# Adaptive layer norm, S4D convolution and a token mixer on one core: where the input's row groups are loaded, when their statistics are taken, and how many products of ones TensorE makes in the first cycle

## The chip, the core and the metric

The kernel runs on one core of one Trainium2 chip. The core has TensorE (PE, the matrix engine), VectorE (DVE), ScalarE (ACT), GpSimd (POOL) and SyncE (SP). SP only issues DMA transfers here, and GpSimd issues some beside its arithmetic. Each engine works through its own list of instructions in order and waits on semaphores for what others make. PE has a second lane in the profile, PEld, for weight loads. The metric is device time in microseconds (us). The kernel before took 697.01 us, the median of three runs (696.69 to 698.48).

## The reference, cut to what matters

```python
x = A_u                                                   # 2048 x 448, fp32
mod = (silu(c) @ w_mod).reshape(1, 6, 1, 448)
sa, ca, ga, sb, cb, gb = six rows of mod
h = layernorm(x) * (1 + ca) + sa
x = x + ga * S4D(h)            # long convolution with a kernel K, by FFT
h = layernorm(x) * (1 + cb) + sb
x = x + gb * mixer(h)          # (W2 gelu(W1 layernorm(h)^T))^T, over the token axis

# S4D: dt = exp(log_dt);  A = -exp(log_A_real) + i A_imag;  C = (C_real + i C_imag) dt
# K[d, l] = 2 Re sum over n of C[d, n] exp(A[d, n] dt[d] l)       d < 448, n < 256, l < 2048
# y = irfft(rfft(h) rfft(K))[:2048] + h D_skip
# mixer: 2048 -> 1792 -> 2048, weights w1 and w2
```

All the change touches is in the first tenth of the run: the first layer norm's statistics of x, and the making of K beside it.

## The kernel before

**Making K.** K is made in 56 steps `s` (28 groups of 16 channels, two halves of the 256 states). A step needs exponents and phases as products of small tables on PE, exponentials and sines of them on ACT, the factors `E` and `G` as elementwise products on DVE and GpSimd, and 64 small products `kg<-E,G` on PE that add them up over the states. Eight steps make a cycle (`BATCH`). A cycle begins with `window(s)`: PE makes the exponents of all eight steps (`xe`, `xg <- tab,lex`, L627) and ACT takes their exponentials (`mag`, L650), one table of functions for all of them. Then each step of the cycle runs `st_step`: ACT takes two absolute values and four sines (L683 to L688), DVE makes `E` in four instructions (L692, L693, L695, L696) and GpSimd makes `G` in two (L690, L691). PE makes the phases of the next step (`st_phase`, L627 with `lph`), and the 64 products of the step before the last (`st_kgen`, L717). The phases stand in two pairs of PSUM banks that DVE reads when it makes `E`, so the phases of step s + 1 wait until `E` of step s - 1 is done. `st_mag2` (GpSimd, L666 and L671) makes a product of magnitudes that `E` reads.

**Before the first cycle** a chain of small instructions on DVE, ACT and GpSimd (`first_chain`) turns the parameters of the first 128 channels into pairs of high and low parts. SP moves them straight into the small tables `lex` and `lph` (`direct`, L885), and also stores them to DRAM (`pars`, L889), from where later groups are loaded (L613, L617). A second chain for the next channels (`chain(1)`) is dealt out in single instructions on DVE (`more`).

**The input.** `x_load(r0, n, eng)` (L306) loads row groups r0 to r0 + n - 1 of x into `xt`, in four transfers of 32 partitions, by the engine given, SP if none is. There are 16 row groups, and each is 224 KB over its four transfers. Row groups 0 to 3 are issued by GpSimd inside `first_chain`, 4 to 7 by SP ahead of the first cycle in two calls of two groups, and 8 to 15 by GpSimd behind steps 1 and 2. `u_stats(r)` (L519, L520) takes mean and variance of row group r on DVE. Groups 0 to 3 are taken inside `window(0)`, the others between the second and third `E` instruction of steps 2 to 7, two in each (`between`). All 16 must be there when `window(8)` computes the scale of the layer norm (`logs(True)`, `u_scale`), from which GpSimd makes `wur` (L535) and PE the first stage of the transform of x (`pu`, L548).

**Other names.** `wm_load(k, tile)` (L331) loads 784 KB of w_mod, and `late[s]` holds loads that SP issues ahead of step s. `modulation` (L504, L508) are PE products on them. `warm(n)` (L639) makes n products of ones on PE into a part of the bank `kg` that nobody reads.

**What sets the order.** PE, ACT, DVE and GpSimd run in the order in which the code is written. So does SP up to step 8. Up to eight of SP's transfers are under way at once, since each waits for the one eight places ahead of it.

Of the kernel before, what the change touches and what calls it, by code (L numbers as in the profile page):

```python
# [30 lines left out]
BATCH = 8  # L31
# [195 lines left out]
def tile_adaln_s4d_mixer(ctx, tc, i, out):  # L227
# [20 lines left out]
    with ExitStack() as es:  # L248
        V, S, G, T = nc.vector, nc.scalar, nc.gpsimd, nc.tensor
# [93 lines left out]
        def wm_slot(k):  # L343
# [3 lines left out]


        late = {
            4: lambda: wm_load(2, wm_slot(2)),  # L350
            7: lambda: wm_load(0, wm_slot(0)),
            6: lambda: [
                nc.sync.dma_start(wu, i["WU"]),
# [309 lines left out]
        def st_mag2(s):  # L663
            me = v32(mags[s][:, 0])
            w = wp.tile([P, GD], F32, tag="w", name="w")
            G.tensor_tensor(w[:, :, None], me[:, :, 31:32], me[:, :, 1:2], ALU.mult)  # L666
            if s in (3, 4, 5):
                m2 = v32(wm0.rearrange("p k d -> p (k d)")[:, -512 * (s - 2) :][:, 0:512])
            else:
                m2 = m2p[s >= 32 and s % BATCH > 2].tile([P, GD, 32], F32, tag="m2", name="m2")  # L670
            G.tensor_tensor(m2, me, w[:, :, None].to_broadcast([P, GD, 32]), ALU.mult)  # L671
            m2s[s] = m2
# [190 lines left out]
        def first_chain():  # L863
            cr, ci, a, aim = (raws[0][nm] for nm in ("A_C_real", "A_C_imag", "A_log_A_real", "A_A_imag"))
            xa, ya, s, t, u, ph, p64 = (
                qp.tile([P, N], F32, tag=nm, name=nm) for nm in ("xa", "ya", "s", "t", "u", "ph", "p64")
            )

            w = xp.tile([P, 2, D], F32, tag="yt", name="first", bufs=3)[:, 0, 0:N]

            def split(eng, src):

                hl = room.pop()
                eng.tensor_copy(hl[:, 0].bitcast(F32R), src)
                eng.tensor_tensor(hl[:, 1].bitcast(F32R), src, hl[:, 0], ALU.subtract)
                return hl

            room = wm0.rearrange("p k d -> p (k d)")[:, -12 * N :].rearrange("p (h j n) -> p h j n", h=6, j=2)
            room = [room[:, h] for h in range(6)]
            signs = room.pop()  # L880
            sr, si_ = signs[:, 0], signs[:, 1]

            def direct(hl, tile, r, g):

                nc.sync.dma_start(tile[g][r : r + 32].bitcast(F32), hl[16 * g : 16 * g + 16])  # L885

            def store(hl, *places):
                for k, v in places:
                    nc.sync.dma_start(pars[0][v, k], hl)  # L889

            S.activation(xa, cr, AF.Abs, scale=0.5)
            S.activation(ya, ci, AF.Abs, scale=0.5)
            S.activation(a, a, AF.Exp, bias=ldt0)
            S.activation(dt[:, 0:1], ldt0, AF.Exp)

            S.activation(one, one, AF.Ln)

            ts(sr, cr, 0.0, 0.5, ALU.is_ge, ALU.subtract)
            ts(si_, ci, 0.0, 0.5, ALU.is_ge, ALU.subtract)
            tt(s, xa, ya, ALU.add)  # L900
            tt(ya, ya, xa, ALU.subtract)
            ts(s, s, 2.0**-120, None, ALU.max)
            V.reciprocal(xa, s)
            ha = split(G, a)
            tt(ya, ya, xa, ALU.mult)
            ts(t, s, 2.0**-40, 2.0**80, ALU.is_lt, ALU.mult)
            stt(p64, t, 1.0, s, ALU.max, ALU.mult)
            for g in range(4):
                direct(ha, lex, 0, g)
                if g < 3:  # L910
                    direct(ha, lex, 64, g)
            par_load(1, par_names[0:2])
            x_load(0, 4, G)
            S.activation(u, ya, AF.Square)
            S.activation(u, u, AF.Ln, bias=1.0)
            S.activation(p64, p64, AF.Ln)
            S.activation(xa, ya, AF.Arctan)
            S.activation(xa, xa, AF.Copy, scale=4 * i2p, bias=-0.5)
            S.activation(dt[:, 1:4], ldt[:, 1:4], AF.Exp)
            S.activation(sc, cvec, AF.Exp, scale=-1.0)  # L920

            ts(dt4[:, 0:1], dt[:, 0:1], 1.0 / (4 * math.pi), None, ALU.mult)
            ts(ldt2[:, 0:1], ldt0, 1.5 * math.log(2.0), None, ALU.add)
            ts(ph, aim, dt4[:, 0:1], None, ALU.mult)
            ts(w, ph, MAGIC, MAGIC, ALU.add, ALU.subtract)
            stt(s, t, -80 * math.log(2.0) / 2.0**80, p64, ALU.mult, ALU.add)
            stt(s, u, 0.5, s, ALU.mult, ALU.add)
            ts(s, s, ldt2[:, 0:1], None, ALU.add)
            hs = split(V, s)
            for g in range(4):  # L930
                direct(hs, lex, 96, g)
                if g == 0:
                    direct(ha, lex, 64, 3)
            tt(ph, ph, w, ALU.subtract)
            hp = split(G, ph)
            direct(hp, lph, 0, 0)

            ts(w, ph, MAGIC7, MAGIC7, ALU.add, ALU.subtract)
            tt(p64, ph, w, ALU.subtract)

            tt(xa, xa, sr, ALU.mult)
            stt(xa, xa, 0.5, si_, ALU.add, ALU.mult)
            stt(xa, ph, 63.0, xa, ALU.mult, ALU.add)
            ts(u, xa, MAGIC, MAGIC, ALU.add, ALU.subtract)
            tt(xa, xa, u, ALU.subtract)
            store(ha, (0, 1), (1, 1))
            hl = split(G, p64)
            direct(hl, lph, 64, 0)
            hc = split(V, xa)
            direct(hc, lph, 96, 0)  # L950
            store(hs, (2, 1))
            store(hp, (0, 0))
            store(hl, (1, 0))
            store(hc, (2, 0))
# [2 lines left out]
        par_load(1, par_names[2:4])  # L957
        for g in (1, 2):
            load(g, False)
        x_load(4, 2)  # L960
        x_load(6, 2)
        wm_load(1, wm_slot(1))
        remainder()

# [44 lines left out]
        def window(s):  # L1009
# [11 lines left out]
            for e in range(BATCH):  # L1021
                st_exp(s + e)

                if e + 1 < BATCH:
                    st_exponents(s + e + 1)
                else:
                    st_phase(s)
                mellow()
                flush(dve)
                flush(act)  # L1030
                if s == 8 and e == 0:
                    tt(mod[1], mod[1], mod[2], ALU.mult)
                if s < 32:
                    more(WPACE[s // 8][e])
                if s == 0 and e >= 4:
                    u_stats(e - 4)
                if s == 8 and e in (3, 4):
                    modulation(0, e - 3)
                if s == 8 and e == 5:

                    G.tensor_tensor(mod[0], mod[0], mod[2], ALU.mult)
                if s and e < (2 if s <= 32 else 1):
                    st_kgen(s - (2 if s <= 32 else 1) + e)
                elif e == 5:
                    if s == 8:
                        yks[0] = y0.tile([P, 32, DC], F32, tag="yk", name="yk0")
                    st_s1(s > 16)

                for k, e0 in ((4, 1), (5, 3), (3, 6)) if s == 16 else ():
                    if e in (e0, e0 + 1):  # L1050
                        modulation(k, e - e0)

                if s == 8:
                    warm(7)
                if s in (8, 16):
                    some(u_rows, rows, (2, 2, 2, 2, 2, 0, 1, 1)[e])
                elif s == 24 and e != 5:
                    some(u_cols, cols, 1)

                if s >= 40 and e == 2:  # L1060
                    piece(False, True)
                if s >= 40 and e == 4:
                    piece(pieces[0] < NP, True)
                if s == 0 and e > 1:
                    st_mag2(e - 2)
                elif s and (e < 2 or s >= 32):
                    st_mag2(s + e)
                if s == 0 and e == 3:
                    for r in range(4):
                        dsk_copy(r)  # L1070
# [10 lines left out]
        for s in range(tail):  # L1081
# [21 lines left out]
            def between():  # L1103
                flush(dve)
                if 2 <= s < BATCH:
                    for r in range(2 * s, 2 * s + 2):
                        u_stats(r)
                if s < len(pace):
                    more(pace[s])
# [5 lines left out]
            else:  # L1115
                if s < 32 and s % BATCH > 1:
                    st_kgen(s - 2)
                if s % BATCH < 2:
                    warm(10)
                if (s + 1) % BATCH:  # L1120
                    st_phase(s + 1)
                elif s + 1 < NHALF:
                    st_exponents(s + 1)
# [8 lines left out]
                st_kgen(s - 1)  # L1132


            if s in (1, 2):
                x_load(4 + 4 * s, 4, G)
            free = s > 7 and not st_s1(s % BATCH == BATCH - 1)
            if s + 2 < 32 and (s + 2) % BATCH > 1 and s + 2 > 5:
                st_mag2(s + 2)
# [325 lines left out]
```

## Time and profile before

| | |
|---|---|
| median of three runs | 697.01 us |
| the profiled execution's own time | 694.39 us |
| its span, first to last instruction | 692.6 us |
| PE busy | 643.8 us (93%) |
| DVE, ACT, POOL busy | 428.5, 451.4, 279.0 us |
| mean granted TensorE clock | 0.989 |

A row of the timeline has a start and a duration in us, the engine, the line of the kernel, the operation, what it writes and reads, how many instructions are merged into the row (x), and in brackets how long the engine had been idle before it and what ended that. "issue" is time in which the profile shows nothing that the engine waited for. A row of waits has a total, how often, and the longest. In a table of stretches stand the busy time of each engine in a stretch, the granted clock, the busy share of the 16 DMA engines and what they moved in GB/s.

### The profile page before, as it was taken

What the parts mean: (1) busy time and instruction counts of PE and PEld (TensorE: products, weight loads), DVE (VectorE), ACT (ScalarE), POOL (GpSimd) and SP (SyncE); (2) the same over time, 40 slices, a digit from 0 to 9 for tenths busy, and PEclk for the clock granted to TensorE, in tenths of its full rate; (3) what the DMA queues carried; (4) which work ended last, traced back from release to release, by engine and by line L of the source; (5) the groups of instructions that cost most, each with busy time, mean ns of one, the idle gap of its engine ahead of it and who ended that gap; (6) DMA issues with size and microseconds to landing.
All of it is one profiled execution on the core that took longest, in us unless ns stands there. A gap on an engine that the chain in (4) does not pass through costs nothing.

```text
span 692.6 us, 18551 instructions
## 1 busy us (share of the span) xinstructions
PE 643.8 (93%) x7332; PEld 487.5 (70%) x7332; DVE 428.5 (62%) x818; ACT 451.4 (65%) x848; POOL 279.0 (40%) x367
## 2 busy tenths in 40 slices
PE   0868999999988899999999999999999999999997
PEld 0444454455445676676789767778899999999996
DVE  7877889787575684857745477776732364444431
ACT  5887698899879899999767578787322352222220
POOL 6694669588488777777568000000000000000000
PEclk9998999999999999999999999999999999999999
DMA  7695647588785585554589699966574445555540
GB/s 181 180 208 134 213 168 239 219 229 272 218 266 166 146 165 162 152 151 120 163 271 358 188 262 251 246 153 162 168 229 112 142 133 160 160 169 166 168 123 27
DMA packets 99496, 128.14 MB, mean 185 GB/s; under 512 B 13518, under 2 KB 79986, under 8 KB 99410
## 3 DMA queue, kind: packets, MB, share of 16 engines
q1 hardware_dynamic: 98210, 123.42, 62.8%
q0 software_dynamic: 1200, 3.54, 2.3%
q8 instruction: 58, 0.95, 0.6%
q14 instruction: 28, 0.23, 0.1%
HBM read 91.57 MB, written 34.87 MB: 183 GB/s over the span
## 4 chain that ended last, share of the span: by engine, by line
PE 72%; ACT 9%; DVE 5%; DMA 4%; issue 4%; POOL 2%; SPq 2%; DVEq 0%; ACTq 0%; POOLq 0%
PE xe L627 8%; PE o L1432 7%; PE o L1431 6%; PE o L1433 6%; PE acc L1270 6%; PE acc L1271 6%; PE acc L1272 6%; PE kg L717 6%; PE xg L627 3%; PE vv L836 3%; PE kx L820 3%; PE vv L837 3%; PE pu L548 3%; PE pu L580 2%; PE kg L639 2%
## 5 line engine op out<-in xcount | busy, mean ns | idle before, releaser
L212 ACT CAST whi<-w 128x896 fp32r<-128x896 f32 x64 | 59.6, 938 | 131.2 <-PE o L1432 82.7
L221 DVE TENSOR_TENSOR wlo<-w,whi 128x896 fp32r<-128x896 f32 x64 | 68.1, 1086 | 40.2 <-ACT whi L212 37.0
L690 POOL TENSOR_TENSOR G<-mag,gs 128x512 f32<-128x512 f32 x56 | 71.9, 1284 | 49.7 <-ACT gs L686 49.7
L1270 PE MATMUL acc<-h3h,whi 128*128 128x448 f32 x224 | 83.0, 371 | 0.7 <-ACT u L1398 0.7
L1271 PE MATMUL acc<-h3l,whi 128*128 128x448 f32 x224 | 81.3, 363 | 0.0
L1432 PE MATMUL o<-ul,whi 128*128 128x448 f32 x224 | 81.3, 363 | 0.0
L1431 PE MATMUL o<-uh,whi 128*128 128x448 f32 x224 | 81.2, 362 | 0.0
L1272 PE MATMUL acc<-h3h,wlo 128*128 128x448 f32 x224 | 80.6, 360 | 0.0
L1433 PE MATMUL o<-uh,wlo 128*128 128x448 f32 x224 | 80.6, 360 | 0.0
L717 PEld LDWEIGHTS kg<-E,G 128*32 128x32 f32 x3584 | 55.4, 113 | 30.4 <-issue 20.0
L691 POOL TENSOR_TENSOR G<-mag,gs 128x512 f32<-128x512 f32 x56 | 71.9, 1283 | 0.0
L717 PE MATMUL kg<-E,G 128*32 128x64 f32 x3584 | 64.8, 225 | 4.8 <-issue 4.0
L627 PE MATMUL xg<-tab,lph 64*128 64x512 f32 x112 | 62.9, 561 | 5.5 <-ACT gs L687 2.9
L627 PE MATMUL xe<-tab,lph 64*128 64x512 f32 x112 | 62.3, 556 | 1.1 <-ACT gs L687 0.9
L692 DVE TENSOR_TENSOR E<-m,xe 128x512 f32<-128x512 f32 x53 | 36.3, 685 | 40.4 <-ACT xe L685 20.4
L1436 DVE TENSOR_TENSOR y<-o,x 128x448 f32<-128x448 f32 x16 | 10.0, 627 | 78.8 <-PE o L1433 78.8
L671 POOL TENSOR_TENSOR m<-mag,w 128x512 f32<-128x512 f32 x53 | 55.8, 1053 | 4.2
L1270 PEld LDWEIGHTS acc<-h3h,whi 128*128 128x128 f32 x224 | 42.0, 188 | 14.2 <-ACT h L1335 4.2
L627 PE MATMUL xe<-tab,lex 64*128 64x512 f32 x56 | 28.7, 527 | 17.5 <-DMA lex<-wm 16.4
L828 DVE TENSOR_TENSOR z<-kx,u 128x448 f32<-128x448 f32 x48 | 28.4, 619 | 26.7 <-PE kx L820 26.7
L1431 PEld LDWEIGHTS o<-uh,whi 128*128 128x128 f32 x224 | 42.1, 188 | 3.1
L1272 PEld LDWEIGHTS acc<-h3h,wlo 128*128 128x128 f32 x224 | 41.9, 187 | 3.1
(242 smaller groups left out, 1531.1 us busy)
## 6 DMA issues: line engine op xcount, KB each, us to landing
w<-in_B_w_dram SPq DMA_DIRECT2D x64, 224.0 KB
w<-in_B_w_dram SPq DMA_DIRECT2D x32, 448.0 KB
yu_d<-yt SPq DMA_DIRECT2D x16, 448.0 KB
yi<-yu_d SPq DMA_DIRECT2D x32, 224.0 KB
us_d<-uo SPq DMA_DIRECT2D x16, 448.0 KB
u<-us_d SPq DMA_DIRECT2D x32, 224.0 KB
v_d<-vt SPq DMA_DIRECT2D x32, 224.0 KB
vt<-v_d SPq DMA_DIRECT2D x14, 448.0 KB
```

Of the source, the lines that this page charges most:

```text
L212: self.nc.scalar.copy(hi, w)
L221: eng.tensor_tensor(lo, w, hi.bitcast(F32), ALU.subtract)
L627: T.matmul(out[k], lhs[r], rhs[r], start=start, stop=stop)
L690: G.tensor_tensor(Gt[:, 1], mg_, v32(sg), ALU.mult)
L691: G.tensor_tensor(Gt[:, 0], mg_, v32(cg_), ALU.mult)
L717: T.matmul(kg[32 * q : 32 * q + 32, m], Gt[:, c, d], E[:, c, d], start=h == 0 and c == 0 and m == 0, stop=h == 1 and c == 1, skip_group_ch ...
L1270: nc.tensor.matmul(acc[f], hi[:, fs], h3h[:, r], start=r == 0, stop=False)
L1271: nc.tensor.matmul(acc[f], hi[:, fs], h3l[:, r], start=False, stop=False)
L1272: nc.tensor.matmul(acc[f], lo[:, fs], h3h[:, r], start=False, stop=r == 15)
L1431: nc.tensor.matmul(o, hi[:, ks], uh[kh][:, k], start=kh == 0 and k == 0, stop=False)
L1432: nc.tensor.matmul(o, hi[:, ks], ul[kh][:, k], start=False, stop=False)
L1433: nc.tensor.matmul(o, lo[:, ks], uh[kh][:, k], start=False, stop=kh == 1 and k == 6)
```

## The change

Row groups 0 to 3 are still loaded by GpSimd, but from inside `window(0)`: the four transfers are issued between the two instructions of `st_mag2(0)`. SP issues groups 4 to 7 and 8 to 11 where it issued 4 to 7, in two calls of four groups, and groups 12 to 15 ahead of step 3, behind a w_mod load that moves there from step 4. GpSimd issues nothing behind steps 1 and 2 any more. The statistics of groups 4 to 15 are taken in other steps: 2, 3, 2, 2, 2 and 1 of them in steps 2 to 7. In steps 2 to 7 PE makes four products of ones between `st_kgen` and `st_phase`, and in the first part of `window(8)` 16 in place of 7.

```diff
--- before.py
+++ after.py
@@ -347,7 +347,7 @@
 
 
         late = {
-            4: lambda: wm_load(2, wm_slot(2)),
+            3: lambda: [wm_load(2, wm_slot(2)), x_load(12, 4)],
             7: lambda: wm_load(0, wm_slot(0)),
             6: lambda: [
                 nc.sync.dma_start(wu, i["WU"]),
@@ -664,6 +664,8 @@
             me = v32(mags[s][:, 0])
             w = wp.tile([P, GD], F32, tag="w", name="w")
             G.tensor_tensor(w[:, :, None], me[:, :, 31:32], me[:, :, 1:2], ALU.mult)
+            if s == 0:
+                x_load(0, 4, G)
             if s in (3, 4, 5):
                 m2 = v32(wm0.rearrange("p k d -> p (k d)")[:, -512 * (s - 2) :][:, 0:512])
             else:
@@ -910,7 +912,6 @@
                 if g < 3:
                     direct(ha, lex, 64, g)
             par_load(1, par_names[0:2])
-            x_load(0, 4, G)
             S.activation(u, ya, AF.Square)
             S.activation(u, u, AF.Ln, bias=1.0)
             S.activation(p64, p64, AF.Ln)
@@ -957,8 +958,8 @@
         par_load(1, par_names[2:4])
         for g in (1, 2):
             load(g, False)
-        x_load(4, 2)
-        x_load(6, 2)
+        x_load(4, 4)
+        x_load(8, 4)
         wm_load(1, wm_slot(1))
         remainder()
 
@@ -1051,7 +1052,7 @@
                         modulation(k, e - e0)
 
                 if s == 8:
-                    warm(7)
+                    warm(7 if e else 16)
                 if s in (8, 16):
                     some(u_rows, rows, (2, 2, 2, 2, 2, 0, 1, 1)[e])
                 elif s == 24 and e != 5:
@@ -1103,7 +1104,7 @@
             def between():
                 flush(dve)
                 if 2 <= s < BATCH:
-                    for r in range(2 * s, 2 * s + 2):
+                    for r in ((4, 5), (6, 7, 8), (9, 10), (11, 12), (13, 14), (15,))[s - 2]:
                         u_stats(r)
                 if s < len(pace):
                     more(pace[s])
@@ -1117,6 +1118,8 @@
                     st_kgen(s - 2)
                 if s % BATCH < 2:
                     warm(10)
+                elif s < BATCH:
+                    warm(4)
                 if (s + 1) % BATCH:
                     st_phase(s + 1)
                 elif s + 1 < NHALF:
@@ -1132,8 +1135,6 @@
                 st_kgen(s - 1)
 
 
-            if s in (1, 2):
-                x_load(4 + 4 * s, 4, G)
             free = s > 7 and not st_s1(s % BATCH == BATCH - 1)
             if s + 2 < 32 and (s + 2) % BATCH > 1 and s + 2 > 5:
                 st_mag2(s + 2)
```

On GpSimd, the end of `first_chain` and the start of `window(0)`. `wm_79` is the room for high and low parts, `ph`, `p_192` and `A_log_A_real` are parameters of the first chain, `mag` holds the exponentials and `m_330` the product that step 0 reads. Before:

```order
L875 TENSOR_TENSOR wm_79<-A_log_A_real,wm_79 128x256
L306 DMA xt<-in_A_u_dram 32x4x448 x4
L874 CAST wm_79<-ph 128x256
L875 TENSOR_TENSOR wm_79<-ph,wm_79 128x256
L874 CAST wm_79<-p_192 128x256
L875 TENSOR_TENSOR wm_79<-p_192,wm_79 128x256
L666 TENSOR_TENSOR w<-mag 128x16
L671 TENSOR_TENSOR m_330<-mag,w 128x512
```

The same place with the change:

```order
L877 TENSOR_TENSOR wm_79<-A_log_A_real,wm_79 128x256
L876 CAST wm_79<-ph 128x256
L877 TENSOR_TENSOR wm_79<-ph,wm_79 128x256
L876 CAST wm_79<-p_192 128x256
L877 TENSOR_TENSOR wm_79<-p_192,wm_79 128x256
L666 TENSOR_TENSOR w<-mag 128x16
L306 DMA xt<-in_A_u_dram 32x4x448 x4
L673 TENSOR_TENSOR m_330<-mag,w 128x512
```

The four loads moved behind two more splits and behind `w` of step 0, which waits for the first exponential of ACT.

On SP, from the loads of x ahead of the first cycle to the loads for the second. `lph` and `lex` are tables of phases and exponents, `pars_57` the parameters stored in DRAM, `wm_79` here the room of w_mod:

```order
-L306 DMA xt<-in_A_u_dram 32x2x448 x8
+L306 DMA xt<-in_A_u_dram 32x4x448 x8
 L331 DMA wm_79<-in_w_mod_dram 112x4x448
 L613 DMA lph_142<-pars_57 32x256
 L617 DMA lph_142<-pars_57 64x1x256
+L331 DMA wm_79<-in_w_mod_dram 112x4x448
+L306 DMA xt<-in_A_u_dram 32x4x448 x4
 L613 DMA lph_143<-pars_57 32x256
 L617 DMA lph_143<-pars_57 64x1x256
-L331 DMA wm_79<-in_w_mod_dram 112x4x448
 L613 DMA lex_145<-pars_57 32x256
```

The eight transfers carry twice the rows. The second w_mod load and four more transfers of x stand ahead of the tables for the second cycle.

## The prediction

> **What bounds the kernel in the part that changes.** I read the stretches first, then the waits, then each engine's timeline from 0 to 75 us. The stretch from the start of the first step (30 us) to the end of the first cycle (68 us):
>
> ```profile
> 30.00:68.00 38.00, 30.64 (x558) 18.45 (x557) 29.81 (x58) 29.85 (x60) 27.02 (x29) 0.87 0.76 176
> ```
>
> The columns are busy us of PE, PEld, DVE, ACT and POOL, granted clock, DMA share, GB/s. No engine is full and PE's clock is 0.87, so waits decide. Of the waits up to 90 us these two fall into that stretch and are its longest on DVE and PE:
>
> ```profile
> DVE st L519 <- DMA xt<-in_A_u_dram: 3.7, 1, 3.7
> ...
> PE kg L717 <- issue: 3.6, 1, 3.6
> ```
>
> DVE's timeline tells which engine paces the eight steps. Each step begins with L692:
>
> ```profile
> 21.74 0.61 DVE L519 BATCH_NORM_STATS2 st<-xt 128x6 f32<-128x448 f32 x1
> ...
> 27.64 0.18 DVE L520 BATCH_NORM_AGGREGATE mv<-st 128x2 f32<-128x6 f32 x1
> 30.66 0.69 DVE L692 TENSOR_TENSOR E<-m,xe 128x512 f32<-128x512 f32 x1 [2.84 <-ACT xe L685]
> ...
> 37.98 0.69 DVE L692 TENSOR_TENSOR E<-m,xe 128x512 f32<-128x512 f32 x1 [0.41 <-ACT xe L685]
> ...
> 41.84 0.68 DVE L692 TENSOR_TENSOR E<-wm,xe 128x512 f32<-128x512 f32 x1
> ...
> 50.65 0.63 DVE L519 BATCH_NORM_STATS2 st<-xt 128x6 f32<-128x448 f32 x1 [3.69 <-DMA xt<-in_A_u_dram]
> ...
> 62.08 0.69 DVE L692 TENSOR_TENSOR E<-m,xe 128x512 f32<-128x512 f32 x1 [1.00 <-issue]
> ...
> 65.34 0.68 DVE L696 TENSOR_TENSOR E<-m,xg 128x512 f32<-128x512 f32 x1
> ```
>
> From 30.66 on DVE stands still three times: 0.41, 3.69 and 1.00 us. A step without a wait is 41.84 - 37.98 = 3.86 us of DVE's work. So DVE is the bound. The cycle lasts 66.02 - 30.66 = 35.36 us, of which 30.26 are DVE's work and 5.10 waits. The 3.69 are for row groups 8 to 11, which GpSimd loads.
>
> PE has a gap and a low clock of its own in that stretch:
>
> ```profile
> 44.02 1.75 PE L717 MATMUL kg<-E,G 128*32 128x64 f32 x64
> ...
> 52.38 0.43 PE L717 MATMUL kg<-E,G 128*32 128x64 f32 x6 [3.62 <-issue]
> ```
>
> The 3.62 lie inside one block of 64 products, with nothing to wait for. In the window from 49 to 51 us an instruction transfer is seen:
>
> ```profile
> q8 instruction: 1, 0.02, 4.1%
> ```
>
> The data queues fill the DMA engines at that time, so I read the gap as PE waiting for its own instructions behind the loads. That is inferred, and a rival hangs on it.
>
> **The change, part by part.** The sizes of the transfers that matter:
>
> ```profile
> xt<-in_A_u_dram POOLq DMA_DIRECT2D x12, 224.0 KB, 9.8
> wm<-in_w_mod_dram SPq DMA_DIRECT2D x3, 784.0 KB
> ...
> pars<-wm SPq DMA_DIRECT2D x6, 256.0 KB
> ```
>
> *Ahead of the first step.* From GpSimd's, SP's and PE's timelines and the chain of waits:
>
> ```profile
> 7.88 2.26 POOL L306 DMA_DIRECT2D xt<-in_A_u_dram  x4
> ...
> 15.32 0.78 POOL L875 TENSOR_TENSOR wm<-p,wm 128x256 fp32r<-128x256 f32 x1
> 17.91 0.24 POOL L666 TENSOR_TENSOR w<-mag 128x16 f32<-128x16 f32 x1 [1.81 <-ACT mag L650]
> ```
>
> ```profile
> 9.12 4.62 SPq L885 DMA_DIRECT2D lex<-wm  x7
> ...
> 16.32 0.33 SPq L285 DMA_DIRECT2D A_C_imag<-in_A_C_imag_dram  x1
> 17.28 3.12 SPq L885 DMA_DIRECT2D lex<-wm  x5
> ```
>
> ```profile
> 16.44 0.76 PE L627 MATMUL xe<-tab,lex 64*128 64x512 f32 x1 [16.44 <-DMA lex<-wm]
> 19.30 0.79 PE L627 MATMUL xg<-tab,lex 64*128 64x512 f32 x1 [2.10 <-DMA lex<-wm]
> ```
>
> ```profile
> 17.28 1.98 DMA lex<-wm
> ```
>
> The small transfers for `lex` go out from 9.12 on, beside the 0.9 MB that GpSimd issued from 7.88. The first lands only at about 16.3, when SP goes on and PE starts: 7 us, against 1.98 for the one at 17.28. With the 0.9 MB gone, SP's seven issues end at 13.74, the two parameter loads behind them take 0.33 each, and the row of `lex` that went out at 17.28 goes out at about 14.5. PE's 19.30 and ACT's first sine move forward by up to 2.8 us; at worst by nothing.
>
> *Where the first rows land.* Landing times of GpSimd's loads, over all twelve, and for those of the first four that were issued after 9 us:
>
> ```profile
> DMA to landing us min/median/max: 4.6/9.8/12.0
> ```
>
> ```profile
> DMA to landing us min/median/max: 6.5/7.0/7.7
> ```
>
> In the new order GpSimd ends its splits at 16.10, makes `w` (0.24) if ACT's first exponential is there, and issues the loads from about 16.5 on, in the same 2.2 us: the last at about 18.2. That one lands after 4.6 us at best (22.8), after 12.0 at worst (30.2). I take 7.7, the slowest of the first four, since they too ran beside SP's loads at the start as these will beside the 1.5 MB of `pars`: 25.9. The first statistics, at 21.74 before, wait until then, and behind them DVE has 27.82 - 21.74 = 6.1 us of work before `E` of step 0. So step 0 starts at 25.9 + 6.1 = 32.0, 1.3 us later than 30.66. The forward move of ACT then gives nothing more, as DVE is last. `m` of step 0, now behind the four loads, is done near 20: nothing.
>
> The rows of issue, and of a cast on DVE beside them in the new order:
>
> ```profile
> L306 POOL DMA_DIRECT2D xt<-in_A_u_dram x12: 550/560/609, 7.9 to 43.5; - x12
> ```
>
> ```profile
> 17.20 0.29 DVE L874 CAST wm<-xa 128x256 fp32r<-128x256 f32 x1
> ```
>
> Here GpSimd's twelve issues took 550 to 609 ns, whatever DVE did. The Trainium skill speaks against this part of the change: "SBUF — State Buffer", section "SBUF: two separate sides", says that GpSimd cannot write the descriptors of its DMAs while DVE runs a copy or cast in a two-port mode. By that rule each of the four loads could start one cast later, an estimate of 4 x 0.29 = 1.2 us in all, and the time would be 694.9. The trace's issue times agree with it at most for the 59 ns between the shortest and the longest.
>
> *The cycle.* With the rows at hand the three waits go: 32.0 + 30.26 = 62.3 against 66.02, a gain of 3.7 us. The moved statistics are the same work in other steps: nothing. What covers them is that the later rows land in time. SP's place for them, and what full queues move:
>
> ```profile
> 30.19 5.54 SPq L306 DMA_DIRECT2D xt<-in_A_u_dram  x8
> ```
>
> ```profile
> 46.00:48.00 2.00, 2.00 (x38) 1.11 (x41) 0.96 (x2) 1.97 (x5) 2.00 (x3) 1.00 1.05 224
> ```
>
> SP gets there near 30 us again, since the tables stored as `pars` come before. It then issues 1.84 MB of x (groups 4 to 11), twice 0.8 MB of w_mod and 0.92 MB of x. At 224 GB/s they land at 38.4, 45.6 and 49.7. Group 8 is now third in step 3. That step starts 41.84 - 30.66 - 0.41 = 10.8 us after step 0, at 42.8, and DVE wants the group at about 45.5. Group 12 is second in step 5, at about 53. The margins are 7 and 3 us; without them up to the old 3.69 come back. The first w_mod load (42) is wanted by PE near 47. The `lex` loads of the second cycle now stand behind the last rows, near 50, ten us before that cycle.
>
> *GpSimd* loses two issues of 2.2 us in steps 1 and 2. It was busy 27 of 38 us and DVE is the bound: nothing.
>
> *Products of ones.* Their prices, what PE does in a step, and its idle time before `pu`:
>
> ```profile
> 32.43 1.26 PE L639 MATMUL kg<-ones 128*128 128x256 bf16 x10
> ...
> 36.36 1.10 PE L717 MATMUL kg<-E,G 128*32 128x64 f32 x64
> ...
> 38.80 1.10 PE L717 MATMUL kg<-E,G 128*32 128x64 f32 x64
> ...
> 46.93 0.96 PE L508 MATMUL pm<-wm,scb 112*32 112x448 f32 x8
> ...
> 67.53 0.94 PE L639 MATMUL kg<-ones 128*128 128x256 bf16 x7
> ...
> 69.99 0.98 PE L548 MATMUL pu<-xt,wur 32*64 32x449 f32 x8 [1.52 <-POOL wur L535]
> ```
>
> Four cost 4 x 126 ns = 0.5 us. A PE step of products and phases is 38.80 - 36.36 = 2.4 us, 2.9 with them, of 3.86: hidden. In steps 4 to 7 the 0.96 of `modulation` fills the rest, so up to 0.3 us in each of four may show, 1.2 in all. They could also gain: a block that takes 1.10 took 1.75 at 44.02, at a low clock, 0.65 us that busy PE would save, if PE were the bound. I take +0.4. The nine more in `window(8)` cost 9 x 134 ns = 1.2 us, inside the 1.52 in which PE waits for `wur`: nothing. Without that cover, 1.2.
>
> *Sum.* -3.7 + 0.4 = -3.3 us. What follows the cycle hangs on the layer norm's scale, which needs the last statistics, so I carry the gain to the end. The profiled execution took 694.39 (span 692.6), 2.6 below the median. So 691.1 for such an execution, 697.01 - 3.3 = 693.7 for the median.
>
> **The rivals.** 0.3%, 2.1 us, is about what a measurement of this kernel can tell from no change.
>
> *The PE stall stays (0.13).* If instructions come late again at the same time, PE's path stays: DVE's step 7 starts at 62.08, when its phases came. It took 3.94 us, now less one statistic of 0.8, and ends at 65.2: a gain of 0.8, 696.2. For it: the DMA engines are as full as before between 30 and 50 us. Against it: PE's next phases wait for DVE until about 51 us anyway, which hides a stall of one or two us, and x leaves the second data queue. The Trainium skill, "DMA: Bandwidth & Descriptors", section "Queues, rings and completion order", says that a DMA engine goes round between its queues packet by packet. By that rule the instructions now take turns with one data queue, not two, and the stall shrinks; no row here shows the turns.
>
> *The first rows come late (0.20; the one on the other side).* DVE's wait at the first statistics is new, and all of its work on step 0 is queued behind it. The cycle ends at the landing + 6.1 + 30.26: no gain from 29.7 on, slower by 0.3% from 31.8. If the `lex` tables come no earlier, `w` stays at 17.91, the last load goes out at 19.9 and at the worst landing, 12.0, is there at 31.9. The cycle then ends at 68.3, 2.2 us later: 699.2. For it: 1.5 MB of `pars` are stored at that time, and the median of all twelve loads is 9.8. Against it: the four at the start landed within 7.7.
>
> *The gain doesn't reach the end (0.07).* A later stage could be held by its loads. Then 697.0.
>
> **How the numbers follow.** The forecast has 0.60: landings from 22.8 to 27.2, gains of 6.9 to 2.1 us, 693.7 as the likeliest; its own range is 690.1 to 694.9. Within 0.3% are the stall (0.13) and the lost gain (0.07), slower the late rows (0.20). So faster 0.60, same 0.20, slower 0.20. The range for 8 in 10 goes from the best landing, 690.0, to just short of the late rows' 699.2: 698.9.
>
> **What would show it.** In the changed profile DVE's wait for `xt` should stand at the first statistics, 3 to 5 us long, with step 0 near 32 and no such wait in steps 2 to 7. The exponents that started at 19.30 should start near 16.5, the cycle's last `E` end near 62 in place of 66, `pu` start near 66 in place of 70, and the clock between 42 and 58 us stay near 1. The forecast fails if the first statistics start after 29.7, if DVE waits for group 8 or 12, or if PE still stands 3 us inside a block of 64.

## The result, and the profile after

The changed kernel took 703.61 us (median of eight runs, 701.76 to 707.71), the kernel before in the same session 696.85. The ratio is 1.011, 95% interval 1.0083 to 1.0137: slower by 1.1%, where I had forecast 0.5% faster. By the ratio the change costs 7.7 us. The two profiled executions lie further apart, 707.71 against 694.39, since the one is 4.1 us above its median and the other 2.5 below. So sizes are taken from the ratios, and places from the traces. Ratios and their intervals, here and below, leave out the few executions that took over 1.5% longer than the fastest of the same kernel; the medians keep them.

Stretches of the changed kernel. The first row answers to the one of 30 to 68 us before; the others cut out what matters in it and behind it:

```profile
30.00:68.00 38.00, 30.52 (x516) 18.24 (x520) 29.60 (x59) 25.94 (x54) 22.81 (x21) 0.87 0.78 165
```

```profile
42.00:46.00 4.00, 3.16 (x72) 2.38 (x73) 3.84 (x9) 2.14 (x5) 1.07 (x1) 0.72 1.06 210
46.00:52.00 6.00, 4.43 (x44) 2.15 (x46) 5.90 (x14) 4.32 (x9) 4.96 (x5) 0.78 1.03 187
52.00:58.00 6.00, 6.00 (x135) 3.85 (x127) 1.30 (x4) 3.10 (x8) 2.90 (x5) 0.83 0.21 65
...
72.00:78.00 6.00, 5.06 (x85) 3.15 (x89) 3.94 (x9) 3.70 (x8) 4.98 (x9) 0.72 0.30 106
...
232.00:240.00 8.00, 7.74 (x89) 4.46 (x82) 1.29 (x2) 5.48 (x11) 5.91 (x11) 0.50 0.87 202
```

PE's granted clock is still 0.87 in the cycle, and it is low in places where it was full before (0.78 from 46 to 52 us and 0.72 from 72 to 78 us, both 1.00 in the kernel before). In the row from 52 to 58 us DVE is busy for 1.30 of 6 us, while the DMA engines are busy to a fifth.

DVE's timeline, with the lines two higher than before (L694 for L692, L698 for L696):

```profile
24.55 0.61 DVE L519 BATCH_NORM_STATS2 st<-xt 128x6 f32<-128x448 f32 x1
...
30.08 0.67 DVE L694 TENSOR_TENSOR E<-m,xe 128x512 f32<-128x512 f32 x1
...
39.99 0.63 DVE L519 BATCH_NORM_STATS2 st<-xt 128x6 f32<-128x448 f32 x1 [1.75 <-DMA xt<-in_A_u_dram]
...
57.98 0.63 DVE L519 BATCH_NORM_STATS2 st<-xt 128x6 f32<-128x448 f32 x1 [4.66 <-DMA xt<-in_A_u_dram]
...
66.28 0.68 DVE L698 TENSOR_TENSOR E<-m,xg 128x512 f32<-128x512 f32 x1
```

DVE does not wait at the first statistics, and step 0 begins 0.58 us earlier than before. But it waits 1.75 us for row groups 4 to 7 and 4.66 us for group 12, so the cycle ends at 66.96 in place of 66.02.

SP's issues, and the two pieces of the chain that ended last which lie in the cycle:

```profile
29.40 6.67 SPq L306 DMA_DIRECT2D xt<-in_A_u_dram  x8
36.74 0.31 SPq L331 DMA_DIRECT2D wm<-in_w_mod_dram  x1
...
39.99 0.32 SPq L331 DMA_DIRECT2D wm<-in_w_mod_dram  x1
41.32 4.40 SPq L306 DMA_DIRECT2D xt<-in_A_u_dram  x4
```

```profile
35.76 9.63 DMA xt<-in_A_u_dram
45.41 12.46 DMA xt<-in_A_u_dram
```

The last quarter of the input is issued until 45.7 and lands at 57.9, 8 us later than the 49.7 of the prediction.

PE's timeline:

```profile
42.84 0.47 PE L627 MATMUL xg<-tab,lph 64*128 64x512 f32 x1 [2.75 <-issue]
...
50.22 1.42 PE L508 MATMUL pm<-wm,scb 112*32 112x448 f32 x8 [1.46 <-DMA wm<-in_w_mod_dram]
...
60.05 0.50 PE L627 MATMUL xg<-tab,lph 64*128 64x512 f32 x1 [1.69 <-DVE E L698]
...
72.94 0.98 PE L548 MATMUL pu<-xt,wur 32*64 32x449 f32 x8 [2.09 <-POOL wur L535]
...
77.63 1.08 PE L548 MATMUL pu<-xt,wur 32*64 32x449 f32 x8
```

The first `pu` starts 2.95 us later than before (72.94 against 69.99), and behind PE's gap of 2.09 us the clock is 0.72 from 72 to 78 us, so that the second `pu` is 4.4 us late. Before, it stood here:

```profile
73.23 0.98 PE L548 MATMUL pu<-xt,wur 32*64 32x449 f32 x8
```

The other part of the loss is far behind the change. The offset of the same ScalarE instruction between the two executions is +4.5 us from 95 to 147 us in the time of the kernel before. It then grows by 1.8 (147 to 151 us, behind 3.4 us at a clock of 0.50), 1.4 (194 to 205), 5.2 (217 to 231, of which 1.4 go again by 241) and 2.8 (241 to 263). In the last two of these places PE stops, which it does not in the kernel before:

```profile
228.43 1.02 PE L719 MATMUL kg<-E,G 128*32 128x64 f32 x57
231.74 0.44 PE L719 MATMUL kg<-E,G 128*32 128x64 f32 x7 [2.29 <-issue]
...
265.97 1.03 PE L757 MATMUL y<-wc,ks 64*64 64x64 f32 x53
269.10 0.69 PE L757 MATMUL y<-wc,ks 64*64 64x64 f32 x11 [2.10 <-issue]
```

Both times PE stops inside a block of 64 products, waiting for nothing that the profile shows, and behind the first stop the clock is 0.50 from 231.5 to 241.7 us (row 232 to 240 above).

### The profile page after: what moved, and what is told of

Same layout as the page of the kernel before. It is cut to its first block, busy times and chain, and to the rows that moved or that the text cites. A ratio compares the mean times of both kernels' runs of the same rounds, so it can differ in the third digit from the quotient of the medians.

```text
span 705.9 us, 18601 instructions
## 1 busy us (share of the span) xinstructions
PE 652.7 (92%) x7365; PEld 492.7 (70%) x7365; DVE 429.6 (61%) x818; ACT 452.0 (64%) x848; POOL 274.6 (39%) x359
## 4 chain that ended last, share of the span: by engine, by line
PE 71%; DMA 9%; ACT 9%; DVE 5%; issue 3%; SPq 1%; POOL 1%; DVEq 0%; ACTq 0%
PE xe L627 7%; PE o L1434 6%; PE o L1433 6%; PE o L1432 6%; PE acc L1271 6%; PE acc L1272 6%; PE acc L1273 6%; PE kg L719 5%; DMA xt<-in_A_u_dram 3%; PE pu L580 3%; PE vv L838 3%; PE vv L839 3%; PE kx L822 3%; PE pu L548 3%; PE kg L639 2%
## 5 line engine op out<-in xcount | busy, mean ns | idle before, releaser
L692 POOL TENSOR_TENSOR G<-mag,gs 128x512 f32<-128x512 f32 x56 | 71.8, 1283 | 59.2 <-ACT gs L688 59.1
L719 PEld LDWEIGHTS kg<-E,G 128*32 128x32 f32 x3584 | 56.3, 114 | 29.4 <-issue 19.3
L694 DVE TENSOR_TENSOR E<-m,xe 128x512 f32<-128x512 f32 x53 | 36.3, 686 | 39.4 <-ACT xe L687 20.5
L685 ACT ACTIVATE ab<-xe 128x512 f32<-128x512 f32 x56 | 33.9, 605 | 18.6 <-PE xg L627 11.5
L1433 PEld LDWEIGHTS o<-ul,whi 128*128 128x128 f32 x224 | 42.0, 188 | 3.2
```

What stands on the lines that cost most here:

```text
L692: G.tensor_tensor(Gt[:, 1], mg_, v32(sg), ALU.mult)
L719: T.matmul(kg[32 * q : 32 * q + 32, m], Gt[:, c, d], E[:, c, d], start=h == 0 and c == 0 and m == 0, stop=h == 1 and c == 1, skip_group_ch ...
L1433: nc.tensor.matmul(o, hi[:, ks], ul[kh][:, k], start=False, stop=False)
```

## The experiments

Three theories. *Landing*: with nearly all the loads in SP's queue, the last rows come late. *Products*: the added products of ones hold up PE. *Code places*: the 33 products add 66 instructions (each product has its weight load) to PE's list, and PE's code is fetched in blocks, so the points where PE waits for its code move through the rest of the program. The offsets below are those of the same instruction in a profiled execution and in that of the kernel before, at the second `pu` where nothing else is said; their places are in the time of the kernel before.

### The parts alone

Products of ones alone:

```diff
-                    warm(7)
+                    warm(7 if e else 16)
...
+                elif s < BATCH:
+                    warm(4)
```

> The kernel before with nothing but the added products of ones (4 in each of steps 2 to 7, 16 in place of 7 in window(8)). Before is taken at 697, the changed kernel at 703.8. If the late landing of rows 12 to 15 makes the loss, this run is at 697 to 698 (at most the 1.2 us of my prediction's bound). If the products themselves hold up PE and the copies of kg that stand behind them, it is at 699 to 701. If the loss comes from the 66 instructions that they add to PE's list (33 products and 33 weight loads), which move the places where PE waits for instructions, it is at 700 to 704, with rows of a PE wait ended by issue inside a block of 64 products somewhere behind 100 us.

701.29 us, ratio 1.0072 (1.0038 to 1.0107). In the trace the second `pu` is 0.9 us *earlier* than before, and the offset stays at -0.5 until 190 us. Between 194 and 231 us it then grows by 6.0, at these rows of PE:

```profile
196.12 0.99 PE L580 MATMUL pu<-yi,s 128*128 128x448 f32 x2 [2.83 <-issue]
...
224.79 0.38 PE L717 MATMUL kg<-E,G 128*32 128x64 f32 x10 [1.78 <-issue]
```

The first of these rows is no new stop. PE waits ahead of the same `pu` in the kernel before:

```profile
195.40 0.99 PE L580 MATMUL pu<-yi,s 128*128 128x448 f32 x2 [1.58 <-DVE E L693]
```

Of the 6.0 us, 1.9 stand around that `pu` and 4.1 around the second row. So what the products do in the first cycle costs nothing, and still the kernel is 5.0 us slower, and its trace loses the time over 120 us behind the last of them. The second row speaks for the code places.

The changed kernel without the products:

> The changed kernel without the added products: the loads and the statistics alone. If the landing makes the loss, it stays near 701 to 704 and DVE waits 4 to 5 us for rows 12 to 15 in step 5. If the products or their instructions make it, it is at 697 or below, whatever DVE waits.

701.37 us, ratio 1.0069 (1.004 to 1.0097). DVE's and PE's timelines:

```profile
39.59 0.63 DVE L519 BATCH_NORM_STATS2 st<-xt 128x6 f32<-128x448 f32 x1 [1.90 <-DMA xt<-in_A_u_dram]
...
57.21 0.63 DVE L519 BATCH_NORM_STATS2 st<-xt 128x6 f32<-128x448 f32 x1 [4.09 <-DMA xt<-in_A_u_dram]
```

```profile
42.43 0.75 PE L627 MATMUL xg<-tab,lph 64*128 64x512 f32 x1 [3.69 <-issue]
...
49.98 1.72 PE L508 MATMUL pm<-wm,scb 112*32 112x448 f32 x8 [1.42 <-DMA wm<-in_w_mod_dram]
```

The same late rows without the products: the second `pu` is 3.1 us late. That is what was expected of the landing.

The first quarter alone (`x_load(0, 4, G)` moved, nothing else):

> The kernel before with nothing but the first quarter of the input moved into the first set; rows 4 to 15 are loaded and counted as before. If that part is a gain, as the exponentials that came 2 us earlier in the changed kernel suggest, it is at 695.5 to 696.5. If issuing from GpSimd beside DVE's casts costs as much as it brings, it is at 697. It tells nothing apart of the other parts, but says what they cost: the sum of the three parts should be 703.8 if they add up.

696.9 us, ratio 0.9995 (0.9969 to 1.0021). The second `pu` is 2.6 us early, and DVE's wait for groups 8 to 11 has shrunk to 1.62:

```profile
47.09 0.63 DVE L519 BATCH_NORM_STATS2 st<-xt 128x6 f32<-128x448 f32 x1 [1.62 <-DMA xt<-in_A_u_dram]
```

The gain is given back between 194 and 222 us in the profiled execution (+0.5 and +2.6), and the times show none. The 2.6 us are no stop. PE works at half its clock there, the first row, where the kernel before, the second row, has the full clock at the same instructions:

```profile
217.00:221.00 4.00, 3.89 (x91) 2.88 (x95) 1.16 (x2) 2.81 (x7) 2.83 (x5) 0.50 0.83 223
```

```profile
217.00:221.00 4.00, 3.34 (x142) 2.41 (x138) 2.65 (x5) 3.97 (x8) 3.25 (x5) 1.00 0.46 123
```

PE's list is that of the kernel before, and its gaps ahead of this place are the same too (0.38, 0.46 and 0.66 us against 0.37, 0.46 and 0.66). So a single execution can lose some 2.6 us by the clock alone, and an offset in one trace is not yet the cost of an edit.

Rows 4 to 15 and their statistics alone (first quarter as before, no products):

> The kernel before with nothing but rows 4 to 15 in SP's queue and their statistics in the new steps; the first quarter stays in the first chain, no products are added. If the landing makes the loss, DVE waits some 4 us for rows 12 to 15 in step 5 and this run is at 701 to 704, with the loss already there at the first pu (near 77 us in place of 73). If it is the products or the instructions, it is at 697 with DVE's wait no longer than the 3.69 it replaces.

702.76 us, ratio 1.0088 (1.0058 to 1.0118). DVE waits 4.51 us for group 12, and the second `pu` is 6.2 us late, again as expected of the landing. With and without the first quarter's move this part costs some 6 us by the second `pu` (6.2 here, 3.1 + 2.6 = 5.7 in the two runs above). By the ratios the parts cost -0.3, +6.1 and +5.0 us; the whole costs 7.7, less than their sum by 3, which the intervals allow.

### Where PE's code ends

33 products of two columns at the start of PE's list, where PE is idle:

```diff
+        for _ in range(33):
+            T.matmul(kg_tile(0)[:, 4, 0:2], ones[:, 0:P], ones[:, 0:2], start=True, stop=True, skip_group_check=True)
         first_chain()
```

> The kernel before with 33 tiny products of ones (two columns each, into the part of the bank kg that nobody reads) at the very start of PE's list, where PE stands idle for over 10 us: the same 66 instructions that the change adds, but no work where anybody waits. If the number of PE's instructions decides where it waits for its own code, the wait inside a block of 64 products near 52 us falls 33 products earlier (x39 left of the block in place of x6), new waits ended by issue stand between 190 and 230 us as in the run with the products of ones alone, and the time is 700 to 702. If those products cost by what they do, this run is at 697 and its waits stand where they stood.

702.15 us, ratio 1.0082 (1.0051 to 1.0113): 66 instructions that delay nobody where they stand (the second `pu` is 0.6 us early) cost as much as the real ones. The wait near 52 us is gone rather than moved, a miss. But this row stands where the run with the real products has its own, at the same product of the same block, and behind it stretches of PE's clock:

```profile
225.25 0.38 PE L717 MATMUL kg<-E,G 128*32 128x64 f32 x10 [2.33 <-issue]
```

```profile
222.00:225.00 3.00, 0.92 (x56) 0.76 (x55) 0.00 (x0) 1.27 (x3) 2.77 (x5) 1.00 1.00 256
225.00:228.00 3.00, 2.43 (x17) 1.35 (x16) 0.00 (x0) 2.27 (x5) 1.25 (x3) 0.67 1.05 193
228.00:231.00 3.00, 3.00 (x69) 2.24 (x68) 0.02 (x1) 2.13 (x5) 2.84 (x6) 0.50 1.08 193
```

While PE stands (222 to 225 us) the DMA engines are full, and one instruction transfer is under way in the window from 222 to 226 us:

```profile
q8 instruction: 1, 0.02, 1.8%
```

The wait of 2.33 us and the clock behind it make 4.5 us of offset, of 6.5 between 194 and 240 us.

The real products and 95 tiny ones, together 256 instructions:

> The kernel before with the added products of ones (alone 701.3) and 95 tiny products at the start: 128 products and as many weight loads, 256 instructions, which is what one 16 KB transfer of PE's code holds by the count of transfers in the profile (58 of them for some 14,700 instructions). If the places where the code ends a transfer decide, everything behind 80 us stands as in the kernel before: no 2.83 and 1.78 us waits ended by issue between 190 and 230 us, and the time is 696.5 to 698. If the products of ones cost by what they do, it stays at 700 to 702.

699.5 us, ratio 1.0026 (0.999 to 1.0061): no difference that can be told, though the median is 1.5 above the expected range, so a cost of the products themselves of up to 0.6% isn't excluded. The places came out as expected: no wait ended by issue between 190 and 240 us, and the offset grows by 0.1 us there (ahead of the `pu` PE waits 1.69 us, close to the 1.58 before). PE's waits of that kind in `kg` are these in the whole execution:

```profile
PE kg L717 <- issue: 1.5, 3, 0.7
```

The changed kernel with 95 tiny ones:

> The changed kernel with 95 tiny products at the start, so that it too has 256 instructions more than the kernel before. If the places of the code decide a part, this run is 3 to 4 us faster than the changed kernel (703.6), near the 701.4 that it takes without the products of ones, at 699.5 to 702. If the products cost by what they do it stays at 703 to 704. If the loads alone made its loss, it stays too.

703.46 us, ratio 1.0068 (1.0035 to 1.01). The median says that nothing was won, the ratio that 0.4% was, against 1.011; the intervals overlap, so the time doesn't decide. In the trace the growth from 205 to 263 us is 1.5 us in place of 6.5, and neither of the changed kernel's two stops is there, as the code places have it. But that execution loses 2.8 us between 194 and 205 in place of 1.4, and 6.2 by the second `pu` in place of 4.4.

64 and 96 tiny products ahead of the kernel before:

> The kernel before with 64 tiny products at PE's start (128 instructions, half of one transfer of PE's code). With 33 it took 702.15, before 697.7. If each extra instruction costs something, 64 take twice the 4.4 us, 706 to 707. If the places decide where the code ends a transfer, the time is another draw between 693 and 703, with waits ended by issue at other places than with 0, 33 and 128, and what they sum to between 0 and 240 us is what the time differs by.

> The kernel before with 96 tiny products at PE's start (192 instructions, three quarters of a transfer). If each extra instruction costs something, 13 us: 710. If the places decide, another draw between 693 and 703, and the wait that stood at 52 us stands 32 products later than in the kernel before (96 of 128 earlier is 32 later): behind its block of 64, in the phases or modulation that follow, or it is gone.

701.14 us, ratio 1.0045 (1.0015 to 1.0075), and 702.62 us, ratio 1.0067 (1.0037 to 1.0098). With 33 it was 1.0082. So the cost isn't proportional to the number: 64 cost no more than 33, and 96 no 13 us. No trace with 64 is read here: the execution that was profiled took 799.03 us, at a granted clock of 0.757. So what was expected of its waits stays untested. With 96 the execution loses 1.8 us near 150 and 2.5 near 220 us, without a row ended by issue there. In both places PE runs at half its clock, for 3.4 us from 145.1 on and for 6.8 from 220.2 on:

```profile
221.00:225.00 4.00, 4.00 (x103) 2.96 (x107) 0.89 (x2) 2.83 (x6) 2.64 (x5) 0.50 0.92 249
```

It is the same kind of loss as with the first quarter alone, so it says nothing of the code places. Of the five counts tried, the kernel before (none) has the lowest median, though 128 can't be told from it.

What shows the code places best is where the stops stand. Count PE's instructions in a trace in order, from 0, weight loads and waits included. The stop inside a block is at number 705 in the kernel before. With the products alone the stops are at 705 and 6593, with 33 tiny products at 6593, and in the changed kernel at 6594 and 7873. All traces but the one with 64 tiny products together have 14 stops of over 0.7 us, ended by issue, inside blocks of products. Divided by 256, every one of their numbers leaves 193 or 194. And each time PE goes on 1.3 to 1.6 us after the record of one 16 KB instruction transfer ends (in the changed kernel 1.30 and 1.41 us). So PE stops where a block of 256 instructions ends and the next one has come late. The waits ahead of the `pu` near 196 us and inside the phases near 42 us don't stand at such numbers.

What stays open is how the 5.0 us divide. The stops and the low clock behind them make 4 to 5 us in three traces, but each is one execution, and half clocks come without stops too.

### What the late rows wait for

Rows 12 to 15 by GpSimd again, the rest as in the changed kernel without the products:

```diff
-            3: lambda: [wm_load(2, wm_slot(2)), x_load(12, 4)],
+            3: lambda: wm_load(2, wm_slot(2)),
...
+            if s == 1:
+                x_load(12, 4, G)
```

> The changed kernel without the added products (701.4), and rows 12 to 15 issued by GpSimd behind step 1 in place of SP in step 3; the second w_mod load stays in step 3. If the late landing of rows 12 to 15 in SP's one queue makes its loss, DVE's wait of 4.1 us for them goes, the first pu starts 3 to 6 us earlier (71 to 74 us in place of 76), and the time is 695 to 698. If it is PE's wait inside the phases near 42 us and the low clock behind it, or w_mod, the wait for the rows may go and the time stays at 700 to 702.

699.17 us, ratio 1.003 (0.9998 to 1.0062), between the two expected ranges. That is 2.7 us less than with them in SP's queue (1.0069, 1.004 to 1.0097), but the intervals overlap, so the time alone doesn't show it. The wait in step 5 is gone, the second `pu` is 0.8 us late in place of 3.1. But the loss isn't gone: groups 4 (1.36 us) and 8 and w_mod are waited for.

```profile
46.43 0.63 DVE L519 BATCH_NORM_STATS2 st<-xt 128x6 f32<-128x448 f32 x1 [1.75 <-DMA xt<-in_A_u_dram]
```

```profile
52.65 1.72 PE L508 MATMUL pm<-wm,scb 112*32 112x448 f32 x8 [2.66 <-DMA wm<-in_w_mod_dram]
```

Rows 12 to 15 in SP's queue, with w_mod's second load behind them (step 4) rather than ahead:

> The changed kernel without the added products (701.4 us), with rows 12 to 15 in SP's queue in step 3 and the second w_mod load behind them in step 4: one load of 784 KB less ahead of these rows. If they are late by the bytes ahead of them, they land 3.5 us earlier (784 KB at 224 GB/s), DVE's wait of 4.1 us in step 5 falls under 1, and the time is 698 to 699.5. If the slow tail decides, in which the DMA engines are busy to a fifth only, DVE still waits 3 to 4 us for them and the time stays at 701 to 702. If the second w_mod load is late instead, PE waits for it in step 6, and the time stays.

700.7 us, ratio 1.0024 (0.9994 to 1.0054), with an interval that again overlaps that of the order before. The group comes 2.2 us earlier (55.05 against 57.21; L520 is the same instruction, one line lower), DVE waits 2.34 and not under 1, and the second `pu` is 0.3 us late. The record names another transfer as the last one:

```profile
55.05 0.63 DVE L520 BATCH_NORM_STATS2 st<-xt 128x6 f32<-128x448 f32 x1 [2.34 <-DMA lex<-pars]
```

The bytes ahead explain a part of the lateness (2.2 us of the expected 3.5). The slow tail may be the rest; no run separates it.

The first quarter moved, and GpSimd's loads of rows 8 to 15 one step earlier:

```diff
-            if s in (1, 2):
-                x_load(4 + 4 * s, 4, G)
+            if s in (0, 1):
+                x_load(8 + 4 * s, 4, G)
```

> The kernel before with the first quarter moved (696.9 us alone) and GpSimd's loads of rows 8 to 15 one step earlier, behind steps 0 and 1: the second data queue stays, PE's list is that of the kernel before. If DVE's remaining wait for rows 8 to 11 (1.62 us at 47.1 in the run with the first quarter alone) is what is left to gain, it goes and the time is 694.5 to 696.5. If the DMA engines' bytes decide, w_mod is late in exchange (PE waits for it from 45 us on), and the time is 696 to 699. If PE's wait for its code near 50 us is what holds the cycle then, DVE waits for PE instead and the time stays at 696 to 698.

700.72 us, ratio 1.004 (1.0009 to 1.007): slower than the kernel before and above all that was expected, and with the first quarter alone it was 0.9995. DVE's wait for group 8 is gone. Group 6 takes 2.36 us in its place, and w_mod pays more:

```profile
53.20 1.72 PE L508 MATMUL pm<-wm,scb 112*32 112x448 f32 x8 [4.84 <-DMA wm<-in_w_mod_dram]
```

```profile
60.15 0.69 DVE L694 TENSOR_TENSOR E<-m,xe 128x512 f32<-128x512 f32 x1 [5.76 <-ACT xe L687]
```

Together the orders show what the first cycle lacks. From 29 us on, 12 row groups of 224 KB and twice 784 KB, 4.36 MB, have to land, 19.5 us at 224 GB/s and so until 49 us at best, and they are wanted between 38 and 53 us. Each order tried leaves at least one load that comes after it is wanted: rows 8 at 50.65 (before) or 47.09 (first quarter alone), rows 12 at 57.98 (changed), w_mod at 52.65 or 53.20. In the orders tried the choice was only who waits; that no order could do better isn't shown. No version tried beats the kernel before by more than the measurement's uncertainty.

## Why the prediction was wrong, step by step

**What bounds the cycle: right.** DVE's work with its waits sets the end: 30.08 + 30.26 + 6.82 of waits (0.41, 1.75, 4.66) = 67.16, within 0.2 us of the cycle's end at 66.96.

**The exponentials come forward: right, and smaller.** The exponents at 19.30 came to 17.42 (16.5 forecast), and a later one waited again, 1.61 us for `lex` at 20.26.

**The first rows: wrong, to the good.** I put their landing at 7.7 us after issue and a wait of 3 to 5 us at the first statistics. They took 5.5 at most, from the row of GpSimd's loads:

```profile
DMA to landing us min/median/max: 3.8/4.8/5.5
```

There was no wait. DVE itself came to them 2.8 us later than before (24.55 against 21.74), partly because of slow instructions beside GpSimd (below). Step 0 began at 30.08, not 32.0. The rival in which they come late had 0.20 and was not it.

**"With the rows at hand the three waits go": the step that failed.** It rested on a landing time by the sum of bytes at 224 GB/s, 49.7 for groups 12 to 15, with a margin of 3 us. They came at 57.9. The sum took the DMA engines as evenly full, at 224 GB/s and for x and w_mod alone, until the last byte. In fact they moved 200 GB/s from 29.4 to 49.7 us, small tables included, where the 4.36 MB of the sum need 215. Then the share of busy time falls to 0.21 and the rate to 65 GB/s from 52 to 58 us with the rows still under way, and SP, with eight transfers out, got to issue the last of them only at 45.7. For groups 4 to 7 I worked out no margin at all. They were wanted at 38.24 (39.99 less the wait), and cost 1.75. The gain of 3.7 became a loss of 0.9 by the cycle's end, and of 4.4 by the second `pu`.

**PE's stall.** "If PE still stands 3 us inside a block of 64" was my test. In the cycle no such stop is left. PE's wait of 2.75 us at 42.84, in the phases, is marked issue too but is of another kind. It ends 0.1 us behind DVE's `E` of step 2, which DVE's wait for row groups 4 to 7 had held up:

```profile
42.06 0.68 DVE L698 TENSOR_TENSOR E<-m,xg 128x512 f32<-128x512 f32 x1
```

The kernel before waits at the same product for the same `E`, 1.69 us until 42.02. With 190 more instructions ahead, in the changed kernel with 95 tiny products, PE waits at that product again (3.81 us until 43.60). So this wait is the landing once more. The stops for code came back at 231.74 and 269.10 us. The rival that kept the stall at its old place had 0.13 and a price of a gain lost; that it could come back elsewhere was not in it.

**Products of ones: right where I looked, wrong in the sum.** In the cycle they cost nothing (+0.4 forecast, -0.9 in the execution with them alone). The cost that counts, 5.0 us of the ratio, is what 66 tiny instructions cost as well (5.7). It comes from the shift of the code, and a cost of the products themselves isn't excluded (up to 0.6% by the run with 256 instructions). I had left the shift out altogether, though I had read the 3.62 us stall as PE's own code coming late. That reading, which the stops' numbers bear out, should have led to the question where the stalls go when the list grows. So it is not true either that all the change touches is in the first tenth of the run.

**"I carry the gain to the end": not borne out.** The first quarter alone gained 2.6 us by the second `pu`, and -0.3 us (interval -2.2 to +1.5) is what the time shows of it. The rival in which a gain is lost behind the cycle had 0.07. It named a later stage held by its loads; in the one trace 2.6 us went to a half clock instead, and whether the gain is lost in every execution the times don't tell.

**The range.** Its better end, 690.1, leaves out the +0.4 for the products, which the other end, 694.9, holds. That changes nothing here.

## What to carry to other kernels

Where the DMA engines are full (a share of 1.0 and more from 34 to 50 us here) until close to the time at which the last load is wanted, expect a new order of the loads to move the wait to another load. Put the landing of the last one at its own issue plus what full queues take from issue to landing (12 us here), not at the sum of bytes, and give a margin to every load, the first one too. An edit that adds instructions to PE's list should be compared with a control that adds as many tiny ones where PE is idle: here that control alone cost 0.8%. And before an edit is blamed for a place where its trace loses time, look at the same place in traces of kernels without that edit: half clocks of 3.4 to 6.8 us came in several executions whatever the edit.

## What the runs showed of the hardware

**PE's code comes in blocks over the same DMA engines as the data.** The profiles count 58 instruction transfers of 16 KB, 0.95 MB, and 59 in the three runs whose lists have 96 or 128 products more. 33 products, real or tiny, made PE stop at the same product near 225 us for 1.78 and 2.33 us, and with 0 or 128 in all it did not stop there. In the changed kernel it stopped within three products of that place, for 2.29 us. All 14 stops stand 193 or 194 instructions behind a multiple of 256, and PE goes on 1.3 to 1.6 us after the record of a transfer ends. The Trainium skill, "Advanced Engine Details and Errata", section "ISA Cache", gives a line of 16 KB, 256 instructions. The count of transfers agrees, and so does the spacing of the stops. Another stop, 2.83 us at the `pu` of 196 us, is no such case: it stood in the last run too (2.86 us), which adds no PE instruction, the kernel before has 1.58 us of it, and in the changed kernel the profile names the load of `s` as what ended it (2.16 us).

**PE's clock was halved for 3.41 us or a multiple of it, and the length of the gap ahead doesn't tell when.** Behind the gap of 2.29 us at 229.4 to 231.7 the clock was 0.50 for 10.24 us; behind 2.33 us it was 0.50 for 6.83 us, from 226.0 on. But behind the 2.83 us that ended at 196.12 (products alone) it stayed 1.00, and with the first quarter alone it was 0.50 for 6.83 us from 216.9 on, with no gap longer than 0.66 us in the 4 us before. The Trainium skill, "TensorE: Matmul & The Clock Gate", section "Part 1: The HAM clock gate (the "warmup" mystery)", puts the slow clock behind an idle window of about 3.4 us. Here it also came behind shorter gaps, and the measurement decides.

**GpSimd slows DVE.** Beside GpSimd's four issues the same cast took 1.07 us (1.08 with the first quarter alone), against 0.29 before:

```profile
17.39 1.07 DVE L876 CAST wm<-xa 128x256 fp32r<-128x256 f32 x1
```

```profile
16.61 2.28 POOL L306 DMA_DIRECT2D xt<-in_A_u_dram  x4
```

The issues took 2.28 us for the four, 2.26 before. The prediction weighed the Trainium skill's rule ("SBUF — State Buffer", "SBUF: two separate sides") that DVE's casts hold up GpSimd's DMAs. The trace shows the other direction: DVE was the one that waited. The same section says that whichever starts first holds the shared port and the other blocks, and with that the row agrees.
